# Padding 64-row operands to 128 rows, equal operand offsets and a division of 576 tokens at 256

## The chip, the cores and the metric

The program runs on one core of a Trainium2 chip. The metric is the device time of one execution in microseconds (us); lower is better. The core has TensorE (PE in the profile, its weight loads PEld), VectorE (DVE), ScalarE (ACT), GpSimd (POOL) and SyncE (SP), which issues all DMAs here.

## What is computed

Three blocks follow each other, all in float32, for 8 batches of 576 tokens:

```python
# linear attention, 8 heads of 64
kv = np.einsum('bhsd,bhse->bhde', k, v)
out = np.einsum('bhsd,bhde->bhse', q, kv)
rms = np.sqrt(np.mean(out * out, axis=-1, keepdims=True) + 1e-06)
x = out / rms * g_norm                      # then (B, S, 512)
# first mixer: U is 576 x 32, V is 32 x 576
h = x.transpose(0, 2, 1) @ U @ V
u = x + h.transpose(0, 2, 1)
z = u + np.maximum(u @ w_ch1, 0.0) @ w_ch2  # 512 -> 2048 -> 512
# second mixer
h = z @ w_in                                # 512 -> 1024, then tanh-gelu
u, v = h[..., :512], h[..., 512:]
v_n = (v - mu) / np.sqrt(var + 1e-06) * g_ln
v_s = np.einsum('ts,bsd->btd', w_sg, v_n) + b_sg[None, :, None]
return z + (u * v_s) @ w_out
```

## The kernel before

Most products are made from a high and a low part of each operand (`three`, L349: high by high, high by low, low by high), so three float32r matmuls stand for one. 576 tokens are five chunks of 128, the fifth with 64 rows (`rows`, L44).

The order on TensorE is that of the code (`manual_schedule`, L134); the orders on VectorE, ScalarE, GpSimd and the DMA queue come from the scheduler when the program is built, and are fixed then. Four stages follow each other.

**Stage 1**, attention beside part of the first product of the first mixer. One batch after the other runs through a list of steps, `PERIOD` (L531; `FIRST`, L532, for the first). Step U is `ch1` (L356): twelve matmuls of 288 columns, one half of the 576 tokens for one slice of `w_ch1`. Step K is `att_kv` (L246) for one pair of heads two batches ahead: per chunk of tokens two float32 matmuls that fill 64 columns of the array each, the fifth chunk from `kvr` with 64 rows. Each float32 matmul appears as two records in the trace, a transposition as one. Step X is `att_x` (L264) for one chunk of the next batch: four float32 matmuls of q by the block matrix `kvbd`, for the fifth chunk with only 64 result rows; ScalarE then takes the square and a copy, VectorE the sum, and after the fifth chunk `att_root` and `att_norm` make the norm. Step T is `att_t` (L307), which multiplies the normed chunk by U. Step D is `att_u` (L324) for one slice of 128 channels of u: the chunks are transposed into two banks of PSUM (two chunks; two and the 64-row one), to each a matmul t4 by v4 is added, ScalarE takes the first bank out and VectorE the second, then `uh` and `ul` are made on ScalarE and VectorE. The PSUM tiles of K, X and D share four buffers (tag `ar`).

**Stage 2** (L583 to L726) makes the rest of the first product by seven products in place of eight (`Unit.product`, L609), with 512 columns a matmul, in the last block 256 (tiles x, y, z; operands T and c).

**Stage 3** (`ch2`, L776) is the second product of the first mixer, 512 columns a matmul (tile acc).

**Stage 4** is the second mixer: `unit_u` (L866) and `unit_v` (L899) make the two halves of h, `unit_s` (L946) the product with `w_sg`, `o_mm` (L975) the one with `w_out`. Tile uso has one half of the tokens in the first 288 columns of a bank and the other half in those of the next bank; each stationary operand is used for both halves. In `unit_s` the fifth chunk of v stands as 64 rows of high and 64 rows of low parts in one tile; it is multiplied by `wgh` with all 128 rows, and its high half by `wgl` with 64:

```python
r = slice(64 * (n % 2), 64 * (n % 2) + 64)
v = (vh, vl)[n % 2][c]
terms = ((v, wgh), (v[r], wgl[r]))
```

Of the kernel before, what the change touches and what calls it, by code (L numbers as in the profile page):

```python
# [12 lines left out]
F32 = mybir.dt.float32  # L13
# [4 lines left out]
ALU = mybir.AluOpType  # L18
# [15 lines left out]
HS = S // 2  # L34
BT = 512
# [8 lines left out]
def rows(c):  # L44
    return P if c < 4 else S - 4 * P
# [14 lines left out]
def tile_kernel(ctx: ExitStack, tc: tile.TileContext, kvm, kvr, qt, gcol, uv, w12,  # L60
# [76 lines left out]

    wa = ctx.enter_context(tc.tile_pool(name="wa", bufs=1, side="left"))
# [25 lines left out]

    def load_kv(b, p):
        if b < 2 and p >= 2:
            x = spare[2 + b][:, (p - 2) * 5 * 2 * P:(p - 1) * 5 * 2 * P].rearrange("p (c k) -> p c k", c=5)
            m, r = x[:, :4], x[:S - 4 * P, 4]
# [4 lines left out]
        nc.sync.dma_start(r, kvr[b, p])  # L173
        kv_t[b, p] = (m, r)

    def load_q(b, p):
        q = ap.tile([P, S], F32, tag=f"q{p}", name=f"q{p}")
        nc.sync.dma_start(q, qt[b, p])
        q_t[b, p] = q
# [84 lines left out]
    def att_x(b, c):  # L264

        n = rows(c)
        if c == 0:
            at_s["ss", b] = small(b, "ss", 0)
            nc.gpsimd.memset(at_s["ss", b][64:, 4], 1.0)
# [9 lines left out]
        nc.scalar.activation(sq[:n], ps[:n], AF.Square)  # L279
        nc.scalar.activation(xn[:n], ps[:n], AF.Copy)  # L280
        nc.vector.tensor_reduce(at_s["ss", b][:n, c], sq[:n], AX.X, ALU.add)
        at_s["x", b, c] = xn
# [9 lines left out]
    def att_norm(b, cs):  # L292

        y = at_s["y", b]
        for c in cs:
            n = rows(c)
            xn = at_s["x", b, c]
            nc.vector.tensor_tensor(xn[:n], xn[:n], y[:n, c].unsqueeze(2).to_broadcast([n, H, D]),
                                    ALU.mult)
# [24 lines left out]
    def att_u(b, d):  # L324


        if d == 0:
            us[b] = [up.tile([P, ND, S], F32R, tag="u32", bufs=2, name=n) for n in ("uh", "ul")]
        t4 = at_s["t4", b]
        ds = slice(d * P, (d + 1) * P)  # L330
        u = mp.tile([P, S], F32, tag="ut", bufs=3, name="ut")
        for o, e, cs in PARTS:
            ps = pm.tile([P, S - 256], F32, tag="ar", bufs=4, name="ups")[:, :e - o]
            for c in cs:
                n = rows(c)
# [4 lines left out]
            if o:  # L340
                nc.vector.tensor_scalar_mul(u[:, o:e], ps, g)
            else:
                nc.scalar.activation(u[:, o:e], ps, AF.Identity, scale=g)
        nc.sync.dma_start(ud[b][:, d], u)
        uh, ul = us[b]
        nc.scalar.activation(uh[:, d], u, AF.Copy)  # L346
        nc.vector.tensor_sub(ul[:, d], u, uh[:, d].bitcast(F32))  # L347
# [135 lines left out]
    nc.gpsimd.memset(kvbd, 0.0)  # L483
    make_identity(nc, ident)
# [37 lines left out]
    for d in range(ND):  # L522
        att_u(0, d)
# [7 lines left out]
    PERIOD = "X0 X1 X2 X3 U X4 U U K0 U K1 U T0 T1 U U T2 T3 U U T4 U K2 U K3 U D0 D1 D2 D3".split()  # L531
    FIRST = "U U K0 U K1 U U U T0 T1 U K2 U K3 T2 T3 U U T4 U U D0 D1 D2 D3".split()  # L532
# [303 lines left out]
    halves = [slice(h * HS, (h + 1) * HS) for h in range(2)]  # L836


    p2["b"] = pb = ctx.enter_context(tc.tile_pool(name="p2b", bufs=1, side="left", reuse_waits="tile"))
# [3 lines left out]
    gl2 = pb.tile([P, ND], F32, tag="gl2", name="gl2")  # L843
# [6 lines left out]
    def halved(t):  # L850
        return t.rearrange("p (h t) -> p h t", h=2)

    def uso():
        return pm2.tile([P, 2, 512], F32, tag="uso", bufs=3, name="uso")
# [44 lines left out]
    def unit_v(n, c):  # L899
# [9 lines left out]
        st = pb.tile([P, 6], F32, tag="st", bufs=2, name="st")  # L909
        mv = pb.tile([P, 2], F32, tag="mv", bufs=2, name="mv")  # L910
# [8 lines left out]
    def norm_v(c):  # L919
# [3 lines left out]
        a, y, q = (pb.tile([P, 1], F32, tag="v" + i, bufs=2, name="v" + i) for i in "ayq")  # L923
# [22 lines left out]
    def unit_s(n, f):  # L946
# [164 lines left out]
```

## Time and profile before

| what | value |
|---|---|
| median of 3 runs | 1377.82 us (1377.21 to 1380.42) |
| profiled execution, first to last instruction (its span) | 1374.1 us, 20734 instructions |
| what lies around the span, against the median | 3.7 us |
| TensorE busy with matmuls | 1341.0 us (98%), 8050 records |
| VectorE, ScalarE, GpSimd busy | 771.7, 535.4, 284.7 us |
| mean granted TensorE clock | 0.996 of full speed |
| stage 1, 2, 3, 4 in the span | 0 to 311.5, to 538.9, to 930.7, to 1374.1 us |

The page gives one execution. Its matmul records overlap, since they are pipelined; what a matmul costs is the distance from its start to the next one's start. The profiled execution's own time is known by its span alone; the runs' median lies 3.7 us above it.

### The profile page before, as it was taken

To read this page: it belongs to the slowest core of one execution; us is meant where nothing else is said; L and a number is where in the kernel's file an instruction comes from. 1 tells how busy PE (TensorE), PEld (TensorE's weight loads), DVE (VectorE), ACT (ScalarE), POOL (GpSimd) and SP (SyncE) were. 2 spreads that over 40 slices of the span, in tenths; PEclk is the share of its full clock that TensorE was granted. 3 is DMA by queue.
4 is the path that set the end of the run, shared out by engine and by line. 5 is a ranking of instruction groups with operands and counts; after the bars stand their busy time and mean duration, and the time that the engine had idled before them with its cause. 6 is when DMAs were issued, how large, how long until landed. Compare 5 with 4: busy or idle time off the path is not lost.

```text
span 1374.1 us, 20734 instructions
## 1 busy us (share of the span) xinstructions
PE 1341.0 (98%) x8050; PEld 1174.8 (85%) x8050; DVE 771.7 (56%) x1405; ACT 535.4 (39%) x888; POOL 284.7 (21%) x268
## 2 busy tenths in 40 slices
PE   6799999999999999999999999999999999999998
PEld 5599999997877789888888888889899999999998
DVE  4767777755765742322232234547676675775874
ACT  4665666654544532311211213445333333323321
POOL 0411001101111000200000001245253452543332
PEclk9999999999999999999999999999999999999999
DMA  9556665355766776835543545531021120110001
GB/s 347 191 190 221 218 214 182 107 180 185 271 221 220 245 261 244 318 93 170 167 144 114 171 161 192 168 108 44 1 70 36 35 70 18 52 53 18 36 18 52
DMA packets 86930, 199.44 MB, mean 145 GB/s; under 512 B 12208, under 2 KB 33456, under 8 KB 85040
## 3 DMA queue, kind: packets, MB, share of 16 engines
q1 hardware_dynamic: 86832, 198.12, 43.2%
q8 instruction: 63, 1.03, 0.3%
q14 instruction: 35, 0.29, 0.1%
HBM read 126.00 MB, written 72.09 MB: 144 GB/s over the span
## 4 chain that ended last, share of the span: by engine, by line
PE 88%; DVE 4%; ACT 1%; DMA 1%; issue 0%; POOL 0%; SPq 0%; DVEq 0%; ACTq 0%
PE acc L350 10%; PE acc L351 10%; PE acc L352 9%; PE uso L962 9%; PE uso L983 7%; PE uso L874 6%; PE c L350 4%; PE c L352 3%; PE c L351 3%; PE y L350 3%; PE y L352 3%; PE y L351 3%; PE v L350 2%; PE v L351 2%; PE v L352 2%; PE xps L272 2%
## 5 line engine op out<-in xcount | busy, mean ns | idle before, releaser
L350 PE MATMUL acc<-yx,w 128*128 128x512 f32 x576 | 224.1, 389 | 0.0
L352 PE MATMUL acc<-yx,w 128*128 128x512 f32 x576 | 224.1, 389 | 0.0
L351 PE MATMUL acc<-yx,w 128*128 128x512 f32 x576 | 224.1, 389 | 0.0
L772 DVE SCALAR_TENSOR_TENSOR yx<-yr,yx 128x1024 fp32r<-128x1024 f32 x70 | 85.8, 1226 | 244.1 <-ACT yx L771 237.1
L771 ACT ACTIVATE yx<-yr 128x1024 fp32r<-128x1024 f32 x70 | 74.3, 1061 | 277.4 <-PE acc L352 264.4
L350 PEld LDWEIGHTS acc<-yx,w 128*128 128x128 f32 x576 | 108.1, 188 | 22.6 <-ACT y L604 0.2
L352 PEld LDWEIGHTS acc<-yx,w 128*128 128x128 f32 x576 | 108.1, 188 | 22.5
L351 PEld LDWEIGHTS acc<-yx,w 128*128 128x128 f32 x576 | 108.1, 188 | 22.2
L350 PE MATMUL c<-uh,w 128*128 128x288 f32 x384 | 116.7, 304 | 0.7 <-ACT uh L346 0.7
L351 PE MATMUL c<-ul,w 128*128 128x288 f32 x384 | 113.6, 296 | 1.8 <-DVE ul L347 1.8
L352 PE MATMUL c<-uh,w 128*128 128x288 f32 x384 | 113.4, 295 | 0.8 <-POOL w L126 0.6
L874 PE MATMUL uso<-zh,wio 128*128 128x288 f32 x512 | 94.2, 298 | 0.6 <-DVE g2u L882 0.4
L983 PE MATMUL uso<-gh,wio 128*128 128x288 f32 x512 | 93.1, 296 | 0.0
L109 POOL TENSOR_TENSOR tmp<-tmp,wior 128x512 int32<-128x512 int32 x12 | 15.7, 1309 | 314.7 <-DVE tmp L108 269.8
L983 PEld LDWEIGHTS uso<-gh,wio 128*128 128x128 f32 x512 | 77.9, 188 | 2.3 <-issue 0.2
L350 PE MATMUL y<-T,c 128*128 128x512 f32 (+1 forms) x200 | 75.3, 376 | 4.1 <-DVE y L602 3.7
L874 PEld LDWEIGHTS uso<-zh,wio 128*128 128x128 f32 x512 | 76.3, 188 | 3.2 <-issue 1.3
L350 PEld LDWEIGHTS c<-uh,w 128*128 128x128 f32 x384 | 72.0, 188 | 4.1 <-issue 1.0
L351 PEld LDWEIGHTS c<-ul,w 128*128 128x128 f32 x384 | 72.1, 188 | 3.8 <-DVE ul L347 2.9
L351 PE MATMUL y<-T,c 128*128 128x512 f32 (+1 forms) x200 | 74.5, 372 | 0.0
L352 PE MATMUL y<-T,c 128*128 128x512 f32 (+1 forms) x200 | 74.5, 372 | 0.0
L352 PEld LDWEIGHTS c<-uh,w 128*128 128x128 f32 x384 | 72.1, 188 | 1.3 <-POOL w L126 0.9
(210 smaller groups left out, 2916.4 us busy)
## 6 DMA issues: line engine op xcount, KB each, us to landing
yr<-yd SPq DMA_DIRECT2D x70, 512.0 KB, 3.7
yd<-y SPq DMA_DIRECT2D x92, 256.0 KB, 3.4
kvm<-kvm_dram SPq DMA_DIRECT2D x28, 512.0 KB, 4.6
raw<-w_dram SPq DMA_DIRECT2D x26, 512.0 KB, 4.2
q<-qt_dram SPq DMA_DIRECT2D x32, 288.0 KB, 4.8
ud<-ut SPq DMA_DIRECT2D x32, 288.0 KB, 2.1
z<-ud SPq DMA_DIRECT2D x8, 1152.0 KB, 6.4
out_dram<-ot SPq DMA_DIRECT2D x31, 288.0 KB, 2.1
```

What stands on the lines that cost most here:

```text
L109: yield behind(nc.gpsimd.tensor_add(t, t, low))
L272: mm(ps[:n, 2 * p:2 * p + 2, :], q_t[b, p][:, c * P:c * P + n], kvbd[:, p, :], start=True, stop=True)
L350: mm(ps, ah, bh, start=start, stop=False, **kw)
L351: mm(ps, ah, bl, start=False, stop=False, **kw)
L352: mm(ps, al, bh, start=False, stop=stop, **kw)
L771: nc.scalar.activation(yh, y, AF.Relu)
L772: nc.vector.scalar_tensor_tensor(yl, y, 0.0, yh.bitcast(F32), ALU.max, ALU.subtract)
L874: mm(ps[:, e, :HS], a[:, s], c[:, halves[e]], start=(d == 0 and i == 0), stop=(d == ND - 1 and i == 2))
L962: mm(ps[:, e, :HS], a[:, s], w[:, halves[e]], start=(c == 0 and i == 0), stop=(c == NC - 1 and i == 1))
L983: mm(ops[d][:, e, :HS], a[:, s], c[:, f, halves[e]], start=(f == 0 and i == 0), stop=(f == ND - 1 and i == 2))
```

## The change

Operands of 64 rows become 128-row ones. `kvr` (and its place in the spare tiles) has 64 rows of zeros below the data, written once by GpSimd; the tiles of q have 64 columns of zeros behind the 576; so `att_kv`, `att_x` and the transpositions of `att_u` take the fifth chunk like the others. In `unit_s` the fifth chunk's second term takes all 128 rows of v by all 128 of `wgl`, whose lower half repeats the upper; it adds low by low, which was left out before.

Tokens are divided at 256 into 256 and 320 columns, not into halves of 288, in `ch1`, `unit_u`, `unit_s` and `o_mm`. A uso tile now takes the last 256 columns of one bank and the first 320 of the next, without a gap.

Offsets: an unused tile of 88 words at the start of the right side of SBUF, a pool for small tiles, and 40 unused words in it move the tiles that follow. In the built program the moving and the stationary operand of each matmul have offsets in their partition. Before, these are equal modulo 64 bytes in all 1728 matmuls of stage 3, and differ by 32 in 660 of the 840 of 512 columns in stage 2 and in all 432 of `unit_v`; in the 288-column ones of `ch1`, `unit_s` and `o_mm` they are equal modulo 64, and in every second one differ by 128 modulo 256; in those of `unit_u` they differ by 32. After it, they are equal modulo 256 in all these matmuls.

Order: `att_u` makes two slices at a time: all ten transpositions into four banks, then the four matmuls t4 by v4, then what takes the banks out. In the list of steps two K stand together, and two D (D0, D2) replace four.

```diff
+CUTS = (slice(0, 2 * P), slice(2 * P, S))
...
+    edge = ctx.enter_context(tc.tile_pool(name="edge", bufs=1, side="right"))
+    nc.gpsimd.memset(edge.tile([P, 88], F32, tag="edge", name="edge"), 0.0)
...
+    rest = [ap.tile([P, 2 * P], F32, tag=f"kvr{i}", name="kvr") for i in range(2)]
+    q_of = [ap.tile([P, NC * P], F32, tag=f"q{p}", name=f"q{p}") for p in range(NP)]
+    for r in rest:
+        nc.gpsimd.memset(r[rows(4):], 0.0)
...
-            r = ap.tile([S - 4 * P, 2 * P], F32, tag="kvr", bufs=2, name="kvr")
+            r = rest[p % 2]
...
-            mm(ps[:n, 2 * p:2 * p + 2, :], q_t[b, p][:, c * P:c * P + n], kvbd[:, p, :],
+            mm(ps[:, 2 * p:2 * p + 2, :], q_t[b, p][:, c * P:(c + 1) * P], kvbd[:, p, :],
...
-        u = mp.tile([P, S], F32, tag="ut", bufs=3, name="ut")
-        for o, e, cs in PARTS:
-            ps = pm.tile([P, S - 256], F32, tag="ar", bufs=4, name="ups")[:, :e - o]
-            for c in cs:
-                n = rows(c)
-                xf = at_s["x", b, c][0]
-                mm(ps[:, c * P - o:c * P - o + n], xf[:n, ds], ident[:n, :n], is_transpose=True,
-                   start=(c == cs[0]), stop=False)
-            mm(ps, t4[:, ds], v4[:, o:e], start=False, stop=True)
...
+        for k in (d, d + 1):
+            for o, e, cs in PARTS:
+                ps[k, o] = pm.tile([P, NC * P - 256], F32, tag="ar", bufs=4, name="ups")
+                for c in cs:
+                    xf = at_s["x", b, c][0]
+                    mm(ps[k, o][:, c * P - o:(c + 1) * P - o], xf[:, k * P:(k + 1) * P], ident,
+                       is_transpose=True, start=(c == cs[0]), stop=False)
+        for k in (d, d + 1):
+            for o, e, cs in PARTS:
+                mm(ps[k, o][:, :e - o], t4[:, k * P:(k + 1) * P], v4[:, o:e], start=False, stop=True)
...
-        t = slice(e * HS, (e + 1) * HS)
-        ps = pm.tile([P, HS], F32, tag="c1", bufs=3, name="c1")
+        t = CUTS[e]
+        ps = pm.tile([P, S - 2 * P], F32, tag="c1", bufs=3, name="c1")[:, :t.stop - t.start]
...
-    PERIOD = "X0 X1 X2 X3 U X4 U U K0 U K1 U T0 T1 U U T2 T3 U U T4 U K2 U K3 U D0 D1 D2 D3".split()
+    PERIOD = "X0 X1 X2 X3 U X4 U U K0 K1 U U T0 T1 U U T2 T3 U U T4 U K2 K3 U U D0 D2".split()
...
+    psm = ctx.enter_context(tc.tile_pool(name="p2s", bufs=1, side="left", reuse_waits="tile"))
+    nc.gpsimd.memset(psm.tile([P, 40], F32, tag="rest", name="rest"), 0.0)
...
-        return pm2.tile([P, 2, 512], F32, tag="uso", bufs=3, name="uso")
+        return pm2.tile([P, 2 * 512], F32, tag="uso", bufs=3, name="uso")[:, 512 - 2 * P:][:, :S]
...
-                for e in range(2):
-                    mm(ps[:, e, :HS], a[:, s], c[:, halves[e]], start=(d == 0 and i == 0),
+                for e in CUTS:
+                    mm(ps[:, e], a[:, s], c[:, e], start=(d == 0 and i == 0),
...
-                r = slice(64 * (n % 2), 64 * (n % 2) + 64)
                 v = (vh, vl)[n % 2][c]
-                terms = ((v, wgh), (v[r], wgl[r]))
+                terms = ((v, wgh), (v, wgl))
```

The place of D on TensorE, between the last U of a batch (tile c) and the first X of the next (tile xps); the matmuls `ups<-ident` are transpositions, `ups<-v` those of t4 by v4. Before, two of the four slices:

```order
L352 MATMUL c_856<-uh,w_646 128x288
L337 MATMUL ups<-ident,xn 128x128 x2
L339 MATMUL ups<-v_119,t_836 128x256
L337 MATMUL ups<-ident,xn 128x128 x2
L337 MATMUL ups<-ident,xn 128x64
L339 MATMUL ups<-v_119,t_836 128x320
L337 MATMUL ups<-ident,xn 128x128 x2
L339 MATMUL ups<-v_119,t_836 128x256
L337 MATMUL ups<-ident,xn 128x128 x2
L337 MATMUL ups<-ident,xn 128x64
L339 MATMUL ups<-v_119,t_836 128x320
```

Now, all four slices:

```order
L364 MATMUL c_853<-uh,w_659 128x320
L344 MATMUL ups<-ident,xn 128x128 x10
L348 MATMUL ups<-v_124,t_833 128x256
L348 MATMUL ups<-v_124,t_833 128x320
L348 MATMUL ups<-v_124,t_833 128x256
L348 MATMUL ups<-v_124,t_833 128x320
L344 MATMUL ups<-ident,xn 128x128 x10
L348 MATMUL ups<-v_124,t_833 128x256
L348 MATMUL ups<-v_124,t_833 128x320
L348 MATMUL ups<-v_124,t_833 128x256
L348 MATMUL ups<-v_124,t_833 128x320
L280 MATMUL xps<-kvbd,q_128 128x128
```

The 64-row transpositions are gone, and the second ten follow when four banks have all been filled.

The same place on ScalarE, where `ut<-ups` takes out a bank, `uh<-ut` makes the high part of u, and `sq<-xps` and `xn<-xps` belong to X. Before:

```order
L343 ACTIVATE ut<-ups,g 128x256 x2
L346 ACTIVATE uh<-ut 128x576
L343 ACTIVATE ut<-ups,g 128x256
L346 ACTIVATE uh<-ut 128x576 x2
L279 ACTIVATE sq<-xps 128x512
L280 ACTIVATE xn<-xps 128x512
L343 ACTIVATE ut<-ups,g 128x256
```

Now:

```order
L355 ACTIVATE ut<-ups,g 128x256 x2
L358 ACTIVATE uh<-ut 128x576 x2
L355 ACTIVATE ut<-ups,g 128x256
L358 ACTIVATE uh<-ut 128x576
L355 ACTIVATE ut<-ups,g 128x256
L287 ACTIVATE sq<-xps 128x512
L358 ACTIVATE uh<-ut 128x576
L288 ACTIVATE xn<-xps 128x512
```

Two `uh` now stand between the second and the third bank's way out.

## Rows read from the trace of the kernel before

**Rows 1.** The page: busy time of each engine, and the chain that ended last.

```profile
PE 1341.0 (98%) x8050; PEld 1174.8 (85%) x8050; DVE 771.7 (56%) x1405; ACT 535.4 (39%) x888; POOL 284.7 (21%) x268
...
PE 88%; DVE 4%; ACT 1%; DMA 1%; issue 0%; POOL 0%; SPq 0%; DVEq 0%; ACTq 0%
```

**Rows 2.** Windows, stage 1 after its start, stage 4: length; busy (x): PE, PEld, DVE, ACT, POOL; clock.

```profile
50.00:311.46 261.46, 256.62 (x2132) 234.81 (x2132) 178.33 (x334) 155.59 (x310) 29.18 (x21) 1.00 0.59 193
...
930.68:1374.10 443.42, 437.82 (x2865) 406.74 (x2863) 300.55 (x645) 147.00 (x235) 180.12 (x176) 1.00 0.12 38
```

**Rows 3.** Windows, columns as in Rows 2: stage 2 (three), units of stage 4, two U.

```profile
485.69:491.14 5.45, 5.45 (x25) 4.50 (x24) 3.46 (x7) 1.83 (x3) 0.58 (x1) 1.00 0.75 276
491.14:505.19 14.05, 14.05 (x61) 11.30 (x60) 5.58 (x8) 7.16 (x12) 1.06 (x1) 1.00 0.67 249
523.54:529.88 6.34, 6.34 (x56) 6.34 (x55) 0.92 (x3) 2.75 (x8) 0.00 (x0) 1.00 0.31 104
1005.79:1018.58 12.79, 12.79 (x97) 12.79 (x96) 10.92 (x27) 4.30 (x7) 9.00 (x10) 1.00 0.34 101
135.49:138.66 3.17, 3.17 (x25) 3.17 (x24) 2.96 (x4) 2.10 (x5) 1.69 (x1) 1.00 0.42 138
```

**Rows 4.** TensorE's timeline at the end of a unit_s (start, length, what, count).

```profile
1149.93 0.69 PE L962 MATMUL uso<-wsgh,vl 128*128 128x288 f32 x4
1150.56 0.53 PE L962 MATMUL uso<-wsgl,vl 64*128 64x288 f32 x2
1151.02 0.50 PE L350 MATMUL v<-wio,zh 128*128 128x512 f32 x1
1151.35 0.39 PE L351 MATMUL v<-wio,zh 128*128 128x512 f32 x1
```

**Rows 5.** TensorE's timeline at one step K; the group of its 128-row records (busy, mean ns).

```profile
144.47 0.29 PE L352 MATMUL c<-uh,w 128*128 128x288 f32 x1
144.69 0.69 PE L255 MATMUL kvps<-kvm 128*64 128x64 f32 x16
...
145.57 0.40 PE L350 MATMUL c<-uh,w 128*128 128x288 f32 x1
145.81 0.30 PE L351 MATMUL c<-ul,w 128*128 128x288 f32 x1
...
L255 PE MATMUL kvps<-kvm 128*64 128x64 f32 x448 | 20.2, 235 | 5.3 <-DMA kvm<-kvm_dram 5.3
```

**Rows 6.** TensorE's timeline, X0 to X3 after a D.

```profile
189.57 1.95 PE L272 MATMUL xps<-kvbd,q 128*128 128x128 f32 x16
191.80 2.05 PE L272 MATMUL xps<-kvbd,q 128*128 128x128 f32 x16 [0.28 <-ACT xn L280]
```

**Rows 7.** TensorE's timeline at the first slice of a D.

```profile
149.93 0.38 PE L337 MATMUL ups<-ident,xn 128*128 128x128 f32 x2
...
150.27 0.58 PE L337 MATMUL ups<-ident,xn 128*128 128x128 f32 x3
150.78 0.41 PE L339 MATMUL ups<-v,t 128*128 128x320 f32 x1
151.03 0.38 PE L337 MATMUL ups<-ident,xn 128*128 128x128 f32 x2
```

**Rows 8.** TensorE's timeline at X4, the fifth chunk's X.

```profile
159.92 0.29 PE L352 MATMUL c<-uh,w 128*128 128x288 f32 x1
160.14 1.09 PE L272 MATMUL xps<-kvbd,q 128*64 128x128 f32 x8
161.16 0.41 PE L350 MATMUL c<-uh,w 128*128 128x288 f32 x1
```

**Rows 9.** ScalarE's instructions by shape: a bank's way out in D.

```profile
L343 ACT ACTIVATE ut<-ups,g 128x256 f32<-128x256 f32 x32 | 15.1, 472 | 5.9 <-PE ups L339 5.5
```

**Rows 10.** Timelines: VectorE's low parts of chunks 2 and 3, and T2 on TensorE.

```profile
135.72 2.41 DVE L304 TENSOR_TENSOR xl<-xn,xh 128x512 fp32r<-128x512 f32 x2
...
138.66 0.40 PE L313 MATMUL tp<-xh,u 128*128 128x512 f32 x1
```

More of the change, by code (lines that the diff above doesn't have):

```diff
@@ L167, in load_kv @@
             x = spare[2 + b][:, (p - 2) * 5 * 2 * P:(p - 1) * 5 * 2 * P].rearrange("p (c k) -> p c k", c=5)
-            m, r = x[:, :4], x[:S - 4 * P, 4]
+            m, r = x[:, :4], x[:, 4]
+            nc.gpsimd.memset(r[rows(4):], 0.0)
         else:
             m = ap.tile([P, 4, 2 * P], F32, tag="kvm", bufs=2, name="kvm")
-            r = ap.tile([S - 4 * P, 2 * P], F32, tag="kvr", bufs=2, name="kvr")
+            r = rest[p % 2]
         nc.sync.dma_start(m, kvm[b, p])
-        nc.sync.dma_start(r, kvr[b, p])
+        nc.sync.dma_start(r[:rows(4)], kvr[b, p])
         kv_t[b, p] = (m, r)
     def load_q(b, p):
-        q = ap.tile([P, S], F32, tag=f"q{p}", name=f"q{p}")
-        nc.sync.dma_start(q, qt[b, p])
-        q_t[b, p] = q
+        nc.sync.dma_start(q_of[p][:, :S], qt[b, p])
+        q_t[b, p] = q_of[p]
     w_raw, wh, wl = {}, {}, {}
@@ L278, in att_x @@
             sq = spare[4][:, 2700:2700 + DM].rearrange("p (h d) -> p h d", h=H)
-        nc.scalar.activation(sq[:n], ps[:n], AF.Square)
-        nc.scalar.activation(xn[:n], ps[:n], AF.Copy)
-        nc.vector.tensor_reduce(at_s["ss", b][:n, c], sq[:n], AX.X, ALU.add)
+        nc.scalar.activation(sq, ps, AF.Square)
+        nc.scalar.activation(xn, ps, AF.Copy)
+        nc.vector.tensor_reduce(at_s["ss", b][:, c], sq, AX.X, ALU.add)
         at_s["x", b, c] = xn
@@ L297, in att_norm @@
             xn = at_s["x", b, c]
-            nc.vector.tensor_tensor(xn[:n], xn[:n], y[:n, c].unsqueeze(2).to_broadcast([n, H, D]),
-                                    ALU.mult)
+            nc.vector.tensor_tensor(xn, xn, y[:, c].unsqueeze(2).to_broadcast([P, H, D]), ALU.mult)
             xf = xn.rearrange("p h d -> p (h d)")
@@ L329, in att_u @@
         t4 = at_s["t4", b]
-        ds = slice(d * P, (d + 1) * P)
-        u = mp.tile([P, S], F32, tag="ut", bufs=3, name="ut")
-        for o, e, cs in PARTS:
-            ps = pm.tile([P, S - 256], F32, tag="ar", bufs=4, name="ups")[:, :e - o]
-            for c in cs:
-                n = rows(c)
-                xf = at_s["x", b, c][0]
-                mm(ps[:, c * P - o:c * P - o + n], xf[:n, ds], ident[:n, :n], is_transpose=True,
-                   start=(c == cs[0]), stop=False)
-            mm(ps, t4[:, ds], v4[:, o:e], start=False, stop=True)
[L340 to L344, printed above, removed]
-        uh, ul = us[b]
-        nc.scalar.activation(uh[:, d], u, AF.Copy)
-        nc.vector.tensor_sub(ul[:, d], u, uh[:, d].bitcast(F32))
+        uh, ul = us[b]
+        ps = {}
+        for k in (d, d + 1):
[8 more added lines that the diff above has]
+                mm(ps[k, o][:, :e - o], t4[:, k * P:(k + 1) * P], v4[:, o:e], start=False, stop=True)
+        u = {k: mp.tile([P, S], F32, tag="ut", bufs=3, name="ut") for k in (d, d + 1)}
+        for k in (d, d + 1):
+            for o, e, cs in PARTS:
+                if o:
+                    nc.vector.tensor_scalar_mul(u[k][:, o:e], ps[k, o][:, :e - o], g)
+                else:
+                    nc.scalar.activation(u[k][:, o:e], ps[k, o][:, :e - o], AF.Identity, scale=g)
+        for k in (d, d + 1):
+            nc.sync.dma_start(ud[b][:, k], u[k])
+            nc.scalar.activation(uh[:, k], u[k], AF.Copy)
+            nc.vector.tensor_sub(ul[:, k], u[k], uh[:, k].bitcast(F32))
     def three(ps, ah, al, bh, bl, start, stop, **kw):
@@ L483, in tile_kernel @@
     nc.gpsimd.memset(kvbd, 0.0)
+    for q in q_of:
+        nc.gpsimd.memset(q[:, S:], 0.0)
     make_identity(nc, ident)
@@ L521, in tile_kernel @@
         load_kv(2, p)
-    for d in range(ND):
+    for d in range(0, ND, 2):
         att_u(0, d)
@@ L835, in tile_kernel @@
     ph1.close()
-    halves = [slice(h * HS, (h + 1) * HS) for h in range(2)]
+    psm = ctx.enter_context(tc.tile_pool(name="p2s", bufs=1, side="left", reuse_waits="tile"))
+    nc.gpsimd.memset(psm.tile([P, 40], F32, tag="rest", name="rest"), 0.0)
     p2["b"] = pb = ctx.enter_context(tc.tile_pool(name="p2b", bufs=1, side="left", reuse_waits="tile"))
@@ L842, in tile_kernel @@
     vt = [slot(6 + h, [2, EH], F32, "vt") for h in range(2)]
-    gl2 = pb.tile([P, ND], F32, tag="gl2", name="gl2")
+    gl2 = psm.tile([P, ND], F32, tag="gl2", name="gl2")
     bs2 = pb.tile([P, S], F32, tag="bs2", name="bs2")
@@ L908, in unit_v @@
         t, v = vt[c % 2][:, 0], vt[c % 2][:, 1]
-        st = pb.tile([P, 6], F32, tag="st", bufs=2, name="st")
-        mv = pb.tile([P, 2], F32, tag="mv", bufs=2, name="mv")
+        st = psm.tile([P, 6], F32, tag="st", bufs=2, name="st")
+        mv = psm.tile([P, 2], F32, tag="mv", bufs=2, name="mv")
         nc.scalar.activation(t, ps, AF.Square, scale=GS)
@@ L922, in norm_v @@
         t, v, mv = vs.pop(c)
-        a, y, q = (pb.tile([P, 1], F32, tag="v" + i, bufs=2, name="v" + i) for i in "ayq")
+        a, y, q = (psm.tile([P, 1], F32, tag="v" + i, bufs=2, name="v" + i) for i in "ayq")
         nc.vector.tensor_scalar_add(a, mv[:, 1:2], 4 * EPS)
@@ L956, in unit_s @@
             else:
-                r = slice(64 * (n % 2), 64 * (n % 2) + 64)
                 v = (vh, vl)[n % 2][c]
-                terms = ((v, wgh), (v[r], wgl[r]))
+                terms = ((v, wgh), (v, wgl))
             for i, (a, w) in enumerate(terms):
-                for e in range(2):
-                    mm(ps[:, e, :HS], a[:, s], w[:, halves[e]], start=(c == 0 and i == 0),
+                for e in CUTS:
+                    mm(ps[:, e], a[:, s], w[:, e], start=(c == 0 and i == 0),
                        stop=(c == NC - 1 and i == 1))
@@ L981, in o_mm @@
             for i, (a, c) in enumerate(((h, gh[n]), (h, gl[n]), (l, gh[n]))):
-                for e in range(2):
-                    mm(ops[d][:, e, :HS], a[:, s], c[:, f, halves[e]], start=(f == 0 and i == 0),
+                for e in CUTS:
+                    mm(ops[d][:, e], a[:, s], c[:, f, e], start=(f == 0 and i == 0),
                        stop=(f == ND - 1 and i == 2))
@@ L994, in o_out @@
     def o_out(n, d):
-        ps = ops.pop(d)[:, :, :HS]
+        ps = ops.pop(d)
         k = 4 * n + d
         last = n == B - 1
-        zs = halved(zsum[d] if last else zl[k].bitcast(F32))
-        to = halved(out[d, :, order[n] * S:(order[n] + 1) * S])
+        zs = zsum[d] if last else zl[k].bitcast(F32)
+        to = out[d, :, order[n] * S:(order[n] + 1) * S]
         tag = dict(tag="g2u", bufs=6) if last else dict(tag="ot", bufs=2)
         o = pb.tile([P, S], F32, name="ot", **tag)
-        for e in (slice(0, 1), slice(1, 2)) if last and d == ND - 1 else (slice(0, 2),):
-            oe = halved(o)[:, e]
+        for e in CUTS if last and d == ND - 1 else (slice(0, S),):
+            oe = o[:, e]
             nc.vector.tensor_add(oe, ps[:, e], zs[:, e])
```

16 lines of the change are left out of this document (6 added, 10 removed).

## The prediction

> **What bounds the kernel now.** First the page's busy times and its chain of waits [rows 1]: TensorE is busy 98% of the span and holds 88% of the chain, and no other engine is over 56%. Then the windows by stage [rows 2]: in stage 1 after its start 256.62 of 261.46 us are matmul time, in stage 4 437.82 of 443.42, with the clock granted at 1.00, so nothing below is a matter of the clock. What TensorE saves is therefore saved in the span as long as no other engine becomes late. The third view is TensorE's timeline: records overlap, so the price of a matmul is the distance from its start to the next start. The windows over stretches without a wait give it [rows 3]: 288 columns cost 12.79/96 = 0.1332 us in stage 4 and 3.17/24 = 0.1321 in a step U, 512 columns 5.45/24 = 0.2271 where the offsets of the two operands are equal and 14.05/60 = 0.2342 where they differ, 256 columns 6.34/54 = 0.1174 (54 of the matmuls start in that window).
>
> The sum is made against the profiled execution's span of 1374.1; the median of the runs, 1377.82, lies 3.7 above it, and I take the saving from the median. The runs lie within 3.2 us of each other; 0.3%, or 4.1 us, is what a measurement can tell from no change.
>
> **The change, part by part.**
>
> *unit_s.* From the four last 128-row matmuls on [rows 4], 149.93 to 151.35 (1.42 us) pass for those four, two of 64 rows and one of 512 columns. Without any switch these would cost 6 x 0.133 + 0.234 = 1.03. So the two switches, into 64 rows and back, cost 0.39, and a 128-row second term removes them. It happens for 8 batches and 4 slices: 32 x 0.39 = **12.5 us**.
>
> *K in pairs.* A K now [rows 5]: 0.22 from the last c to the first record, 0.88 to the next c, 0.24 to the one after; less two c at 0.133 this is 1.07 us. The 128-row records go at (20.2/28 - 0.235)/15 = 0.032 us each (28 steps of 16). A double step is 40 records all of one kind: 0.22 + 40 x 0.032 + 0.24 - 0.27 = 1.47, against 2.14. The 24 K of the periods become 12 pairs, each 0.67 less: **8.0 us**. K1 and K3 run one U (3.17/2 = 1.6 us) earlier; nothing waits behind them for long, since the only waits of K for a DMA, 5.3 us in all, are in the program's first microseconds, and the loads are two batches ahead.
>
> *att_u without 64-row transpositions.* A transposition or a 128-column matmul of q follows the one before at (1.95 - 0.29)/15 = 0.111 us [rows 6]. A slice's second part takes 150.27 to 151.03 = 0.76 [rows 7]; the first, with one 128-row transposition and 64 columns less, takes 0.34. Without a switch the second would take 0.34 + 0.11 + 0.03 = 0.48: 0.28 saved in each of 32 slices, **9.0 us**.
>
> *Fifth att_x.* At X4 [rows 8] the entry costs 160.14 - 159.92 - 0.133 = 0.09 more than a c, and inside 1.02 - 8 x 0.111 = 0.13 is over. 0.22 x 7 periods = **1.5 us**.
>
> *Offsets.* The two 512-column distances of [rows 3] are of the same program lines and operand kinds and differ by 0.0071 us. Times the 660 + 432 matmuls that become equal: **7.8 us**; between 0 (if the difference is something else of those stretches) and that. For the 288-column ones I take nothing, since every row of them holds both kinds of offset.
>
> *256 and 320.* No row shows a stream of 320 columns. Between 256 at 0.1174 and 512 at 0.2271 a straight line gives 0.1448; the pair 0.2622 against 0.2664 (stage 4) and 0.2642 (U). 1216 pairs x 0.0042 + 576 x 0.0020 = **6.3 us**. The one 320-column matmul in a timeline, 150.78 to 151.03 [rows 7], has 0.25, with the return from 64 rows in it. From below: at the 512's price per column the pair is 0.2555 and the saving 18 us. From above: if 320 costs 0.147 to 0.150 it is 0, or a loss of 4. I take the line, as the 256 row and the 512 row are both near.
> The Trainium skill ("TensorE: Matmul & The Clock Gate", section "Back-to-back issue gap") gives the gap as the columns at the clock plus a fixed part. By it 256 + 320 costs what 288 + 288 does and this term is 0; the trace agrees that a fixed part exists, but its 256 and 512 do not lie on one line with its 288.
>
> GpSimd gets about fifteen small fills before its first real work and is busy 21% of the span [rows 1]: nothing.
>
> Gross: 12.5 + 8.0 + 9.0 + 1.5 + 7.8 + 6.3 = 45 us.
>
> **What is given back.** (a) Four banks. D2's first transposition needs the bank that ScalarE takes out first. The first t4 by v4 starts behind ten transpositions, after some nine distances of 0.111, at 1.0 us; its record is a little under the 0.41 of the 320-column one [rows 7], ScalarE's way out 0.47 [rows 9]: 1.9 us, while TensorE is done with D0 at 1.6. So 0.3 waits in D, and, with two uh now ahead of the third way out on ScalarE, some 0.5 between X0 and X2 against the 0.28 that stands there now [rows 6]: 0.5 more in each of 7 periods, 3.5. (b) The chain from X4 over sum, root, norm and xl to T2 has 138.66 - (135.72 + 2.41) = 0.53 of slack [rows 10]. TensorE will be at T2 about 1.0 earlier (K 0.67, X4's exit, D0): 0.4 of it waits, 2.8. (c) The start and the last D, where c follows D directly and waits for ul: 2.5. (d) Stages 2 and 4, where 1 to 2% of the time TensorE waits for others already [rows 2]: 2. Together about 11, an estimate with 5 on either side. Net 34: **1344 us** (own range 1336 to 1352).
>
> **Rivals.**
>
> *A longer piece is cheaper than the line says.* 256 and 320 both at the rate per column of 512: another 12 us, 1332. For: one row alone has 256. Against: it lies clearly above that rate (0.1136). 0.10.
>
> *Stage 1 becomes bound by ScalarE and VectorE.* They are busy 155.59 and 178.33 of 261.46 [rows 2], but in serial chains. Then T and the banks of D wait as long as TensorE is early, the 8.0 + 9.0 + 1.5 of stage 1 are given back but for the (a) and (b) already counted, 6.3: another 12, so 1356. For: slack in (b) is only 0.53. Against: twelve steps U a period lie between, which can stand in. 0.13.
>
> *Columns alone count.* A matmul in a stream costs by its columns, whatever the offsets and the division; both terms, 14, fall away: 1358. Against: 0.2342 and 0.2271 for the same columns [rows 3]. 0.08, a half of it for the offsets alone (1352). The Trainium skill ("TensorE: Matmul & The Clock Gate", section "Step-by-step: what each phase is for") has the streaming and the stationary operand on two independent read ports, which speaks for it; the trace disagrees as far as these two rows go.
>
> *The change does not do what it says:* the gaps at 64 rows are not from the switch but from the dependence on what comes next, and 128 rows keep them. Then unit_s, att_u and X4, 23 us, give nothing, and some 3 of what is given back goes with them: 1364. Against: the same gap stands at four different places. 0.04. The Trainium skill ("TensorEngine Tiling (Array Packing)", section "When to Use Tiling") would rather go the other way, with 64-row tiles side by side; no run here shows two side by side, and the two 64-row matmuls of unit_s, 150.56 to 151.02, take longer than two of 128 rows.
>
> *Slower:* the 320-column piece costs far more than the line, as where the next weight load, now behind a 256 and then a 320, is late. Without the cuts the net gain is 34 - 6.3 = 27.7; the pairs now cost 476 us in all (1216 x 0.2664 + 576 x 0.2642), so the gain is gone when a pair costs 0.281, a 320-column piece 0.164. At the 0.25 of [rows 7] it would be 1792 x 0.105 = 188 more, 1532. Against: 0.25 there holds the switch. 0.03.
>
> **How the numbers follow.** 0.62 for the forecast, the rest as above. The predicted time is the forecast's, 1344. The range 1331 to 1358 reaches to the first rival below and to the third above, and leaves out the last two and tails of the others. Faster by over 0.3%: all but the last rival and part of one case: 0.95; same 0.02, slower 0.03.
>
> **What would show it right or wrong.** In the profile of the changed kernel: in the timeline of unit_s no 64-row record, and 0.13 or 0.26 from start to start to its end; K as one block of 40; D as ten transpositions and four matmuls in 1.6 us, then a wait of 0.3 for ScalarE; T2 waiting for VectorE's xl; 0.227 for 512 columns everywhere in stage 2 and unit_v; 0.262 for a pair of 256 and 320; stage 3 unchanged in length, stage 1 shorter by about 9, stage 2 by 4, stage 4 by 20. Wrong, if pairs of 256 and 320 cost 0.266 or more, if stage 2 keeps 0.234, or if the waits in stage 1 grow by more than 10 us.

## The result, and the profile after

The changed kernel takes 1354.66 us (median of 4 runs, 1354.00 to 1357.06) against 1378.59 us for the kernel before in the same comparison: a ratio of 0.9832, with a 95% interval of 0.9820 to 0.9845, or 23 us less by the ratio. The profiled execution has a span of 1353.4 us. Forecast were 1344 us: the direction and the range hold, the gain is two thirds of the 34 us.

The page's busy times, and the windows of stage 1, stage 2 and stage 4 (columns as in [rows 2]):

```profile
PE 1311.8 (97%) x8050; PEld 1172.6 (87%) x8050; DVE 773.2 (57%) x1405; ACT 533.5 (39%) x888; POOL 287.2 (21%) x272
```

```profile
50.46:306.29 255.83, 244.97 (x2132) 232.30 (x2132) 181.64 (x340) 153.74 (x310) 29.06 (x16) 0.99 0.60 198
306.29:530.72 224.43, 218.08 (x1052) 182.40 (x1051) 130.13 (x185) 104.79 (x178) 26.40 (x16) 1.00 0.69 234
...
922.95:1353.37 430.42, 424.12 (x2865) 405.30 (x2863) 301.17 (x645) 146.74 (x235) 180.81 (x176) 1.00 0.12 39
```

TensorE is still the bound. Against the stage limits of before, stage 1 ends 5.2 us earlier (forecast 9), stage 2 is 3.0 shorter (4), stage 3 half a us longer, stage 4 13.0 shorter (20). In stage 1 TensorE's busy time fell by nearly 12 us, but the stage by only half of that: where 4.8 us were not busy in [rows 2], 10.9 are now.

The end of a unit_s now, the place of [rows 4] (TensorE's timeline):

```profile
1136.11 0.70 PE L974 MATMUL uso<-wsgh,vl 128*128 128x256 f32 x4
1136.64 0.43 PE L974 MATMUL uso<-wsgl,vl 128*128 128x256 f32 x2
1136.91 0.39 PE L362 MATMUL v<-wio,zh 128*128 128x512 f32 x1
1137.14 0.40 PE L363 MATMUL v<-wio,zh 128*128 128x512 f32 x1
```

1.03 us from the first to the last of these starts where it was 1.42: the term's 0.39 to the digit. A pair of K now, against one K in [rows 5]:

```profile
141.60 0.31 PE L364 MATMUL c<-uh,w 128*128 128x320 f32 x1
141.84 0.69 PE L265 MATMUL kvps<-kvm 128*64 128x64 f32 x16
142.35 0.29 PE L265 MATMUL kvps<-kvr 128*64 128x64 f32 x4
142.47 0.64 PE L265 MATMUL kvps<-kvm 128*64 128x64 f32 x16
142.93 0.29 PE L265 MATMUL kvps<-kvr 128*64 128x64 f32 x4
143.15 0.38 PE L362 MATMUL c<-uh,w 128*128 128x256 f32 x1
143.37 0.28 PE L363 MATMUL c<-ul,w 128*128 128x256 f32 x1
```

1.77 us from the first start to the last; less a c of 320 (0.147) and one of 256 (0.120) this is 1.50 (forecast 1.47) where two K took 2.14. A D, and what follows:

```profile
146.44 1.25 PE L344 MATMUL ups<-ident,xn 128*128 128x128 f32 x10
147.45 0.77 PE L348 MATMUL ups<-v,t 128*128 128x256 f32 x4
148.38 1.32 PE L344 MATMUL ups<-ident,xn 128*128 128x128 f32 x10 [0.17 <-ACT ut L355]
149.46 0.77 PE L348 MATMUL ups<-v,t 128*128 128x256 f32 x4
150.39 2.44 PE L280 MATMUL xps<-kvbd,q 128*128 128x128 f32 x17 [0.16 <-ACT ut L355]
```

From start to start two slices take 1.94 and 2.01 us, or some 0.98 a slice, where [rows 7] had 1.10 and the step forecast 0.82 without a wait. Behind both pairs TensorE waits for a bank that ScalarE takes out. What a pair takes without that wait shows at the last D, whose second pair has a c behind it:

```profile
282.79 1.32 PE L344 MATMUL ups<-ident,xn 128*128 128x128 f32 x10 [0.16 <-ACT ut L355]
283.86 0.78 PE L348 MATMUL ups<-v,t 128*128 128x256 f32 x4
284.47 0.28 PE L362 MATMUL c<-uh,w 128*128 128x256 f32 x1
```

1.68 us, where the step had 1.64 (twice 0.82). So 0.26 of the 1.94 and 0.33 of the 2.01 are waits; 0.3 was forecast for the first. The brackets show less, 0.17 and 0.16, since they count from the modelled end of the record before.

The division of the tokens, in the timeline of a U, at the change from 256 to 320 columns, and in windows over two U and over 48 matmuls of a uso tile:

```profile
144.56 0.28 PE L364 MATMUL c<-uh,w 128*128 128x256 f32 x1
144.68 0.31 PE L362 MATMUL c<-uh,w 128*128 128x320 f32 x1
144.83 0.31 PE L363 MATMUL c<-ul,w 128*128 128x320 f32 x1
```

```profile
169.60:172.80 3.20, 3.20 (x26) 3.20 (x25) 2.25 (x3) 0.61 (x2) 2.06 (x2) 1.00 0.44 96
...
1160.00:1166.40 6.40, 6.40 (x49) 6.36 (x48) 5.34 (x15) 2.51 (x4) 5.77 (x10) 1.00 0.29 92
```

256 columns go at 0.12, 320 at 0.147. A pair costs 3.20/12 = 0.267 in U and 6.40/24 = 0.267 in stage 4. Forecast was 0.2622; before it was 0.264 and 0.266 [rows 3]. The term of 6.3 us is not there.

### The profile page after: what moved, and what is told of

Read it like the earlier page. It is cut to its first block, busy times and chain, and to the rows that moved or that the text cites. A ratio compares the mean times of both kernels' runs of the same rounds, so it can differ in the third digit from the quotient of the medians.

```text
span 1353.4 us, 20742 instructions
## 1 busy us (share of the span) xinstructions
PE 1311.8 (97%) x8050; PEld 1172.6 (87%) x8050; DVE 773.2 (57%) x1405; ACT 533.5 (39%) x888; POOL 287.2 (21%) x272
## 3 DMA queue, kind: packets, MB, share of 16 engines
q8 instruction: 63, 1.03, 0.3%
## 5 line engine op out<-in xcount | busy, mean ns | idle before, releaser
L362 PE MATMUL c<-uh,w 128*128 128x320 f32 (+1 forms) x384 | 116.8, 304 | 1.0 <-ACT uh L358 1.0
L364 PE MATMUL c<-uh,w 128*128 128x320 f32 (+1 forms) x384 | 114.2, 297 | 2.2 <-POOL w L127 2.2
L363 PE MATMUL c<-ul,w 128*128 128x320 f32 (+1 forms) x384 | 114.9, 299 | 1.2 <-DVE ul L359 1.1
L887 PE MATMUL uso<-zh,wio 128*128 128x256 f32 (+1 forms) x512 | 93.1, 297 | 1.3 <-DVE g2u L895 1.3
L994 PE MATMUL uso<-gh,wio 128*128 128x256 f32 (+1 forms) x512 | 93.2, 296 | 0.0
L887 PEld LDWEIGHTS uso<-zh,wio 128*128 128x128 f32 x512 | 79.1, 190 | 2.0 <-PE uso L974 1.7
L362 PEld LDWEIGHTS c<-uh,w 128*128 128x128 f32 x384 | 73.5, 192 | 2.4 <-ACT uh L358 1.2
L364 PEld LDWEIGHTS c<-uh,w 128*128 128x128 f32 x384 | 73.5, 191 | 2.4 <-POOL w L127 2.4
```

Source lines behind the costliest of these rows:

```text
L362: mm(ps, ah, bh, start=start, stop=False, **kw)
L363: mm(ps, ah, bl, start=False, stop=False, **kw)
L364: mm(ps, al, bh, start=False, stop=stop, **kw)
L887: mm(ps[:, e], a[:, s], c[:, e], start=(d == 0 and i == 0), stop=(d == ND - 1 and i == 2))
L994: mm(ops[d][:, e], a[:, s], c[:, f, e], start=(f == 0 and i == 0), stop=(f == ND - 1 and i == 2))
```

## The experiments

Each was compared with the kernel before, run beside it; "by the ratio" means the ratio times 1378 us. The changed kernel stands at 0.9832. In the code cuts, "..." stands for lines left out.

**s_only.** One line of the kernel before:

```diff
...
-                terms = ((v, wgh), (v[r], wgl[r]))
+                terms = ((v, wgh), (v, wgl))
```

> The kernel before with one edit: in unit_s the fifth chunk's second term takes all 128 rows. Theory (the switch to 64 rows and back costs 0.39 us at each of 32 places): 12.5 us faster than before, 1366. Rival (the gap belongs to the fifth chunk or to what comes next, not to the 64 rows): within 2 us of before, 1377 to 1379. In the profile the theory expects a unit_s of 28 distances of 0.133 = 3.73 us where before has 4.01, and 0.1 less at the first distance behind it.

1366.69 us, ratio 0.9921 (0.9908 to 0.9935): 10.9 us. The end of a unit_s there:

```profile
1146.56 0.69 PE L961 MATMUL uso<-wsgh,vl 128*128 128x288 f32 x4
1147.09 0.43 PE L961 MATMUL uso<-wsgl,vl 128*128 128x288 f32 x2
1147.36 0.39 PE L350 MATMUL v<-wio,zh 128*128 128x512 f32 x1
1147.59 0.40 PE L351 MATMUL v<-wio,zh 128*128 128x512 f32 x1
```

The same 1.03 us as in the changed kernel. The 64 rows made the gap; the rival falls. The interval of the ratio, 9.0 to 12.7 us, holds the 12.5.

**pad_only.** Only the padding of stage 1; the lists of steps, the slices one by one, halves, offsets and unit_s as before (the uso tile alone has no gap, as in the changed kernel):

```diff
...
-            r = ap.tile([S - 4 * P, 2 * P], F32, tag="kvr", bufs=2, name="kvr")
+            r = rest[p % 2]
...
-            mm(ps[:n, 2 * p:2 * p + 2, :], q_t[b, p][:, c * P:c * P + n], kvbd[:, p, :],
+            mm(ps[:, 2 * p:2 * p + 2, :], q_t[b, p][:, c * P:(c + 1) * P], kvbd[:, p, :],
...
-                mm(ps[:, c * P - o:c * P - o + n], xf[:n, ds], ident[:n, :n], is_transpose=True,
+                mm(ps[:, c * P - o:(c + 1) * P - o], xf[:, d * P:(d + 1) * P], ident,
...
```

> Of the change only the padding in stage 1: kvr, q and the transpositions with 128 rows; K and D one by one as before, halves of 288, old offsets, unit_s with 64 rows as before. Theory (the switches to 64 rows are the gain in stage 1: 24 K x 0.24 = 5.8, 28 to 32 slices x 0.28 = 7.8 to 9.0, X4 1.5 us, together 15 to 16, and 3 to 6 of it given back as waits): 9 to 13 us faster than before, 1365 to 1369. Rival (stage 1 is bound by ScalarE and VectorE, and nearly all is given back): 1373 to 1378.

1365.42 us, ratio 0.9908 (0.9891 to 0.9924): 12.7 us, at the upper end. In its trace stage 1 after its start takes 249.4 us, some 12 less than before, and each later stage lies within 0.5 us of before. So most of the 15 to 16 stays, and the rival that stage 1 is bound by ScalarE and VectorE falls.

**single_k** and **single_d.** Of the changed kernel, the K one by one; or the slices of D one by one, where att_u has the loop of before (transpositions into two banks, a t4 by v4 behind each, one slice a call) with 128 rows. The list for the first batch changes in the same way:

```diff
-    PERIOD = "X0 X1 X2 X3 U X4 U U K0 K1 U U T0 T1 U U T2 T3 U U T4 U K2 K3 U U D0 D2".split()
+    PERIOD = "X0 X1 X2 X3 U X4 U U K0 U K1 U T0 T1 U U T2 T3 U U T4 U K2 U K3 U D0 D2".split()
...
```

```diff
...
-    PERIOD = "X0 X1 X2 X3 U X4 U U K0 K1 U U T0 T1 U U T2 T3 U U T4 U K2 K3 U U D0 D2".split()
+    PERIOD = "X0 X1 X2 X3 U X4 U U K0 K1 U U T0 T1 U U T2 T3 U U T4 U K2 K3 U U D0 D1 D2 D3".split()
...
```

> The changed kernel with the K one by one again, a U between them, all still with 128 rows. Theory (most of K's 8.0 us came from the switch between 128 and 64 rows inside K, and a pair saves only one entry and one exit, 0.09 + 0.10 us each way beside the c): 2 to 3 us slower than the changed kernel, 1356.5 to 1358. Rival (the pairing is what saves): 6 to 8 us slower, 1361 to 1363.

> The changed kernel with att_u one slice at a time, in the order of before (transpositions into two banks, a t4 by v4 behind each), with 128 rows throughout; four D in the list of steps. Theory (the switches gave the gain, the pairing only makes TensorE wait for the banks): 2 to 5 us faster than the changed kernel, 1350 to 1353, with a D of 3.3 us in place of 3.9. Rival (the pairing itself saves, since going from transpositions to t4 by v4 and back costs): 1 to 5 us slower, 1356 to 1360.

single_k: 1357.28 us, ratio 0.9846 (0.9832 to 0.9859), 1.9 us slower than the changed kernel by the ratio, with intervals that overlap; the rival, 6 to 8 us, falls. A K of its timeline:

```profile
142.67 0.31 PE L364 MATMUL c<-uh,w 128*128 128x320 f32 x1
142.91 0.69 PE L265 MATMUL kvps<-kvm 128*64 128x64 f32 x16
...
143.87 0.28 PE L363 MATMUL c<-ul,w 128*128 128x256 f32 x1
```

1.20 us from the last c to the second one behind K; less the two c this is 0.93, where [rows 5] gave 1.07 and a pair has 1.50 for two. So on TensorE the rows save 24 x 0.14 = 3.4 us and the pairs 12 x 0.36 = 4.3, and that most of K's 8 us came from the rows, as the theory had it, does not hold. Less than 4.3 reaches the time, and more is waited for in turn: in stage 1 after its start TensorE is not busy for 8.3 us in single_k and for 10.9 in the changed kernel.

single_d: 1351.96 us, ratio 0.9802 (0.9789 to 0.9815), 4.1 us **faster**. Two of its slices in the timeline:

```profile
145.12 0.38 PE L343 MATMUL ups<-ident,xn 128*128 128x128 f32 x2
145.25 0.36 PE L345 MATMUL ups<-v,t 128*128 128x256 f32 x1
145.46 0.49 PE L343 MATMUL ups<-ident,xn 128*128 128x128 f32 x3
145.70 0.40 PE L345 MATMUL ups<-v,t 128*128 128x320 f32 x1
145.93 0.38 PE L343 MATMUL ups<-ident,xn 128*128 128x128 f32 x2
```

One slice takes 0.81 us, as the step had it for a slice without a switch. Going from a transposition to a t4 by v4 and back costs nothing here (a pair without its wait has 0.84 a slice). The pairing gives nothing to TensorE, and its waits for a bank make D some 0.17 a slice longer. The seven D of stage 1 and the X0 to X3 behind six of them take 51.6 us in the changed kernel and 47.6 in single_d: 4.0 of the 4.1 us.

**halves.** The changed kernel with one cut moved (and the place of the uso tile with it):

```diff
-CUTS = (slice(0, 2 * P), slice(2 * P, S))
+CUTS = (slice(0, HS), slice(HS, S))
...
```

> The changed kernel with the tokens divided into halves of 288 again, all else as in it (operands' offsets too, but that every second matmul differs by 128 modulo 256). As the prediction had it (256 and 320 save 6.3 us): 1361. Theory after the changed kernel's trace (a matmul costs its columns and a fixed part, so the pair costs 0.266 either way, and 0.264 for halves in step U): 0 to 2 us faster than the changed kernel, 1352.5 to 1355. Third way (the 128 modulo 256 costs as the 32 modulo 64 did): over 1358.

1353.95 us, ratio 0.9826 (0.9812 to 0.9839): 0.8 us faster by the ratio, less than can be told from no change. Two U there take

```profile
169.90:173.07 3.17, 3.17 (x26) 3.17 (x25) 2.09 (x3) 0.60 (x2) 2.03 (x2) 1.00 0.42 98
```

3.17 against 3.20. The 128 modulo 256 that halves bring back costs nothing either, at 288 columns.

**cut192.** The same line with 192 in place of 256:

```diff
+CUTS = (slice(0, 192), slice(192, S))
...
```

> The changed kernel with the tokens divided at 192 into 192 and 384. If a matmul costs its columns and a fixed part however short it is (from 320 and 512 columns, 0.1491 and 0.2267 us: 0.404 ns a column and 0.020; from the pairs: 0.0133 each): the pair is 0.266 to 0.267 and the time stays, 1354 to 1356. If a short matmul cannot start sooner than its 128-column weight load allows, as the 0.111 us of the 128-column matmuls of X suggest: 192 costs 0.111, 384 some 0.174, the pair 0.285, 1792 x 0.0185 = 33 us slower, 1386 to 1390. Straight line of the prediction (each piece by a line through 256 and 512): 192 costs 0.09, 384 some 0.172, the pair 0.262, 1347.

1443.35 us, ratio 1.0472 (1.0456 to 1.0488). The step from 192 to 384 columns in a U:

```profile
77.32 0.27 PE L364 MATMUL c<-uh,w 128*128 128x192 f32 x1
77.43 0.36 PE L362 MATMUL c<-uh,w 128*128 128x384 f32 x1
77.62 0.34 PE L363 MATMUL c<-ul,w 128*128 128x384 f32 x1
77.80 0.34 PE L364 MATMUL c<-uh,w 128*128 128x384 f32 x1
```

192 columns cost 0.11, as the second theory had it (its reason, the weight load, is not shown by this), 384 some 0.18 in these rows (0.174 is the median over the U's). That explains 33 of the 88 us beyond the changed kernel. For the rest the waits table shows TensorE in stage 4 behind VectorE (its table: what waited for what, total, times, longest):

```profile
PE uso L887 <- DVE ot L1015: 13.6, 5, 3.8
PE uso L974 <- DVE ot L1015: 9.2, 2, 5.3
```

and a mean granted clock of 0.976. The orders on the other engines are made anew with each program; why they fit so badly here was not followed.

**no_align** and **align_only.** The changed kernel without its unused tiles and its pool for small tiles; the kernel before with them alone:

```diff
-    edge = ctx.enter_context(tc.tile_pool(name="edge", bufs=1, side="right"))
-    nc.gpsimd.memset(edge.tile([P, 88], F32, tag="edge", name="edge"), 0.0)
...
-    psm = ctx.enter_context(tc.tile_pool(name="p2s", bufs=1, side="left", reuse_waits="tile"))
-    nc.gpsimd.memset(psm.tile([P, 40], F32, tag="rest", name="rest"), 0.0)
...
```

> The changed kernel without the unused tiles and the pool for small tiles, so that the offsets of stage 2, unit_u and unit_v stand as before (differing by 32 modulo 64). Theory (0.0071 us for each 512-column matmul of unequal offsets, 1092 of them, and something in unit_u): 7 to 10 us slower than the changed kernel, 1362 to 1365, with 0.234 from start to start in stage 2. Rival (the stretches differ by something else): 1354 to 1356 and 0.227.

> The kernel before with the unused tiles and the pool for small tiles alone, so that offsets in stage 2 and unit_v become equal. Theory (0.007 us for each of 1092 matmuls, of which 2 to 3 us in stage 2 turn into waits for VectorE): 4.5 to 6 us faster than before, 1371.5 to 1373.5, with 0.227 from start to start in stage 2. As the prediction had it: 7.8, 1370. Rival (offsets bring nothing): 1377 to 1379.

no_align: 1359.10 us (1356.14 to 1362.59), ratio 0.9864 (0.9847 to 0.9881), 4.4 us slower than the changed kernel by the ratio. align_only: 1374.22 us, ratio 0.9969 (0.9960 to 0.9978), 4.3 us faster than before. The same 166 matmuls of 512 columns in stage 2, in windows of the changed kernel and of no_align:

```profile
321.02:358.67 37.65, 37.65 (x168) 31.16 (x166) 20.94 (x31) 19.68 (x32) 4.93 (x3) 1.00 0.66 230
```

```profile
323.64:362.48 38.84, 38.84 (x168) 31.26 (x166) 21.02 (x31) 19.71 (x32) 4.93 (x3) 1.00 0.65 221
```

37.65/166 = 0.2268 and 38.84/166 = 0.2340: the rate forecast, from offsets alone. It is their difference that counts, not the place of one operand: in the built program of before, the 180 matmuls of 512 columns in stage 2 with equal offsets have both operands at 32 bytes modulo 64, and they go at 0.227. But only some 4.4 us arrive. Part of the rest is a wait of y for VectorE in stage 2: 3.7 us before, and with the offsets equal

```profile
PE y L362 <- DVE y L616: 5.6, 5, 1.3
```

in the changed kernel (5.1 us in align_only).

**last.** The changed kernel with one more U between X4 and T0, and one less before D, in the last batch that has X:

```diff
+    LAST = "X0 X1 X2 X3 U X4 U U U U U T0 T1 U U T2 T3 U U T4 U U D0 D2".split()
...
-        for s in PERIOD if b else FIRST:
+        for s in LAST if b == B - 2 else PERIOD if b else FIRST:
```

> The changed kernel with one more U between X4 and T0, and one less before D, in the last batch that has X (there no K stands between them). Theory (TensorE waits 1.05 and 0.64 us for ScalarE and VectorE at T0 there, and the granted clock then falls): the waits go, 1.5 to 3.5 us faster than the changed kernel, 1351 to 1353. Rival (what TensorE waits for is late whatever stands between, so the wait moves to T2, T4 or D): within 1 us of the changed kernel, 1354 to 1356.

The place in the changed kernel, in TensorE's timeline and in a window over it:

```profile
264.74 0.51 PE L320 MATMUL tp<-xh,u 128*128 128x512 f32 x1 [1.05 <-ACT xh L310]
265.88 0.50 PE L322 MATMUL tp<-xl,u 128*128 128x512 f32 x1 [0.64 <-DVE xl L311]
```

```profile
264.70:272.00 7.30, 6.62 (x30) 5.84 (x31) 4.13 (x7) 2.73 (x6) 0.00 (x0) 0.77 0.09 30
```

No K stands there, so the chain from X4 to T0 has less cover than in other batches. 1353.06 us (1351.68 to 1357.39), ratio 0.9819 (0.9802 to 0.9836): 1.8 us by the ratio, with intervals that overlap. In its profile the wait of T0 in that batch is gone, and 0.2 us is left for xl, so the waits did not move on. As to time this is inconclusive.

**best2.** Slices one by one, halves, and the list of the last experiment, together:

```diff
-CUTS = (slice(0, 2 * P), slice(2 * P, S))
+CUTS = (slice(0, HS), slice(HS, S))
...
-    PERIOD = "X0 X1 X2 X3 U X4 U U K0 K1 U U T0 T1 U U T2 T3 U U T4 U K2 K3 U U D0 D2".split()
+    PERIOD = "X0 X1 X2 X3 U X4 U U K0 K1 U U T0 T1 U U T2 T3 U U T4 U K2 K3 U U D0 D1 D2 D3".split()
+    LAST = "X0 X1 X2 X3 U X4 U U U U U T0 T1 U U T2 T3 U U T4 U U D0 D1 D2 D3".split()
...
```

> The changed kernel with three things together: att_u one slice at a time with 128 rows, tokens in halves of 288, and one more U before T0 in the last batch. If the three are independent: 3 to 4, 0.7 and 1.5 to 3.5 us faster than the changed kernel, 1347 to 1350. If stage 1 is by then bound by ScalarE and VectorE: no better than the first alone, 1351 to 1352.5.

1348.67 us (1347.06 to 1350.47), ratio 0.9782 (0.9769 to 0.9795), where the interval of the changed kernel begins at 0.9820. The three are about independent: 4.1 + 0.8 + 1.8 = 6.7 by the ratios, and 6.9 came.

## Why the prediction was right, and where it was not

By the ratios, the parts that were run apart give: padding in stage 1 -12.7 us, K in pairs -1.9, slices in pairs +4.1, unit_s -10.9, offsets -4.3, the division +0.8. The sum is -24.9, and the change measured as a whole is -23. The 1.9 us between the two lie within the intervals; the pairs and the division were taken out of the changed kernel, the other parts put into the kernel before. The 1354.7 us lie nearer to the times of the second and the third rival (1356, 1358) than to the forecast's 1344, so the time alone would not have told which came true, and that the range holds it is in part luck.

- **unit_s**, forecast 12.5: 10.9. The 0.39 at each place is exact, and 12.5 lies in the interval of s_only.
- **K, att_u and fifth att_x**, forecast 18.5 in all, 8.8 of it given back under (a) to (c): net 9.7, measured 12.7 + 1.9 - 4.1 = 10.5. A K pair, a single slice and a pair of slices without its wait (1.68 for 1.64) cost what the steps said. What the pairing of slices costs is the wait for ScalarE of (a), which was sized too small: in each of six periods D waits 0.58 us (3.94 from D0 to X0, less twice 1.68), and X0 to X3 take 0.9 us more in all than before; 4.4 together, where (a) had 0.5 a period. The gain that the diff's pairing of slices seems to promise was in the 128 rows, and the pairing gives back a third of it.
- **Offsets**, forecast 7.8: 4.3 to 4.4. The price of a matmul was right; more than the 2 us under (d) were given back. For matmuls of 256 and 320 columns (unit_u in no_align, 0.266 to 0.267 a pair) no gain shows.
- **256 and 320**, forecast 6.3: -0.8. This is the step that failed, and 7 of the 11 us by which the forecast missed. That a pair costs 0.267 is also the first of the signs that the prediction named for being wrong. It drew a straight line from 256 columns (0.1174) to 512 (0.2271), and the two ends do not belong together. The 0.2271 was read where offsets are equal; of the 210 matmuls of 256 columns in stage 2, 180 have offsets that differ by 32 modulo 64 in the built program of before, and none in that of the changed kernel. The 54 of [rows 3] take there

```profile
515.08:521.56 6.48, 6.48 (x57) 6.48 (x55) 0.85 (x2) 2.75 (x8) 0.00 (x0) 1.00 0.30 102
```

6.48/54 = 0.1200. All eight runs with the unused tiles have this; the four without have 0.1174 (before, pad_only) or 0.1187 (s_only, no_align). A line from 0.1200 to 0.2268 gives 0.1467 for 320 columns and 0.2667 for the pair, as measured, and 1792 pairs multiplied the difference. Why 256 columns go 1 to 3 ns faster at the old offsets is not shown. At the granted clock of 1.00, the higher of the two levels, 2.4 GHz, 512 columns are 0.2133 us and cost 0.2268; 576 columns in two pieces are 0.240 and cost 0.2667 as 256 and 320 and 0.264 to 0.2667 as halves. Each matmul has its columns and 0.012 to 0.014 us. The prediction's bound from above was off as well: by its own 0.1174, 320 columns at 0.147 still save 2.3 us, and at 0.150 they lose 3. The Trainium skill ("TensorE: Matmul & The Clock Gate", section "Back-to-back issue gap") has this form, columns at the clock and a fixed part, for the gap of an isolated matmul; the trace agrees with the form, with 13 ns for its 2.5 ns.
- **Given back**: forecast 11, of it 8.8 in stage 1. In the waits table of stage 1 after its start TensorE now waits 10.7 us, where it waited 4.8 (the table, too, counts from modelled ends). Of (b), 2.8, some 1.2 came: VectorE's xl is waited for 1.6 us, where it was 0.4. The largest single wait was not on the list: the first batch's c waits 2.2 us, where it waited 0.6, for a weight part that GpSimd makes, since TensorE reaches it earlier (it goes on at 66.8 us, before at 66.9). In some periods X waits a us for a bank whose way out waits for the u that an earlier slice still has to send:

```profile
185.92 0.55 DVE L353 TENSOR_SCALAR ut<-ups,g 128x320 f32<-128x320 f32 x1 [1.65 <-DMA ud<-ut]
...
186.52 2.05 PE L280 MATMUL xps<-kvbd,q 128*128 128x128 f32 x16 [1.04 <-DVE ut L353]
```

Of the rivals, one half of "columns alone count" came true, that the division does nothing, and the other half did not: equal offsets are worth 0.0072 us a matmul. On the offsets the Trainium skill ("TensorE: Matmul & The Clock Gate", section "Step-by-step: what each phase is for") would expect no such thing from two independent read ports; the two windows above disagree with it. That stage 1 is bound by ScalarE and VectorE, that the gap is not from the 64 rows, and that 320 columns cost 0.164 or more, are shown false by pad_only, s_only and the timeline. A fourth buffer for u, which might take away the wait for its transfer, was not tried.

## What to carry to other kernels

A switch of the matmul's rows is worth more than the rows: padding a 64-row operand to 128 removed from 0.14 us (a K) to 0.39 (unit_s) at a place and was most of this gain. Price a new size of matmul from columns at the granted clock and a fixed part that several sizes confirm, all under the same conditions: here the one end of the line had unequal offsets and the other equal ones. The same columns in as many pieces cost the same here, until a piece was short (192). When a change puts two things together, test them apart: here the padding paid, and the pairing that came with it took a third of that back.

## What the runs showed that was not expected

- Equal offsets of the two operands make a 512-column matmul 7 ns shorter (0.2340 to 0.2268), where before they differed by 32 bytes modulo 64. A difference of 128 modulo 256 was run with 288 columns alone, where it costs nothing (halves).
- The same change makes the 256-column matmuls of stage 2 longer, from 0.1174 or 0.1187 to 0.1200.
- A stream of 192-column matmuls goes no faster than one of 128-column ones: 0.111 us each (cut192; [rows 6] for 128, where each is one of the two records of a float32 matmul).
- After the two waits at T0, 1.05 and 0.64 us, the window that follows has a granted clock of 0.77, so a part of it at 1.2 GHz. The profiles of halves and single_d have waits in the same place and 1.00 there, so it does not follow each time; in that of no_align a stretch of 3 us behind the wait has 0.50.
